# Attention and MLP gradients in one kernel: one masked GpSimd product for the block diagonals, GpSimd preparation, and a third pair of PSUM banks in the last stage

## The chip, the cores and the metric

The kernel runs on one core of a Trainium2 chip. The metric is the device time of one execution in microseconds (us). The times of before are the median of five runs, 505.92 us; the single runs lie between 502.8 and 509.14. The profile is of one more execution, and its instruction times are used below.

The core's engines work on queues of their own and meet only through semaphores. PE is the matrix engine (PEld its weight loads), DVE is VectorE, ACT is ScalarE, POOL is GpSimd, and SP here only issues transfers. Matrix results land in PSUM, eight banks of 2 KB per partition; DVE or ACT must move them to SBUF ("evacuate") before a transfer can write them out.

## The reference

One decode step with two sequences: x is layer-normed, attention over a cached K and V (16 key heads, 32 query heads, 4096 positions of 128) and a gated bilinear MLP run side by side, and their sum with x is the output. The kernel also returns the gradients with respect to x, K, V and the five weights, for a given gradient dy of the output:

```
xn  = (x - mean) / sqrt(var + eps)
q   = xn wq;  p = softmax(q K^T / sqrt(128));  o = p V
out = x + o wo + ((xn w_gate) * (xn w_up)) w_down
```

The large outputs are sums of a few outer products. For one sequence and key head, dV is p^T (dy wo^T) over the two query heads of that key head, and dK is ds^T q with ds the gradient of the scores: 4096 x 128 elements, each a sum of two products. The weight gradients are outer products with two terms, one per sequence: wq from xn and dq (out_4), wo from o and dy (out_5), and the three of the MLP (out_6 to out_8). As much is written as is read: 92.48 MB each way.

The gradient with respect to x passes back through the layer norm with the row sums of dxn and dxn * xn; it and the output are two rows of 576 elements.

## The kernel before

The key heads are taken in four groups of four. A group has four steps (two sequences by two pairs of heads), so there are 16 steps. A step loads two K heads and two V heads of 1 MB each (`kv` tiles of the pool tag `nat`, 12 buffers), transposes them on DVE (tile `X`), forms scores on PE in `ps_sc`, takes the softmax, forms dscores, and contracts with K and V. Beside this run the nine slices of the MLP (`mlp_units`), a few units per step, and at the end of each group `back_units` with the group's weight gradients.

The dK and dV outputs come from `outer_units`. Per head there are four units; a unit fills a pair of PSUM banks with two matmuls of 128x512 and evacuates them into a quarter of a 1 MB tile `so`, and after the fourth POOL issues the write of that tile. The stationary operand is a masked product: `masked` multiplies the rows of p or ds by a 0/1 mask into 128x1024 (`prm`, `dsm`) in one POOL product. The moving operand is the block diagonal `bd`, 128 x (2, 4, 128): partition block a holds `dense` in its place a and zeros elsewhere. `build_bd` makes it: a small matmul, an ACT copy to `dense` (L511), and four POOL copies of 32 partitions (L516) into one of three tiles that were set to zero once at the start (L229 to L231).

PSUM is divided by tags: `m` (two small tiles), `sc` (two tiles for the scores), and `o` (two pairs of banks, `ps_o`, L80). Every outer product of the kernel takes a pair `ps_o` and is evacuated by `evac` (L104), which keeps a running estimate of the load of DVE and ACT and gives each evacuation to the engine that would be done first; `dve()` and `act()` add the estimates of other work. Evacuations have the line L109 on DVE and L112 on ACT, all blocked matmuls the line L93.

The order of the work is that of the program text, filled in by a scheduler that moves instructions of lower priority between those of the main chain; on each engine the order is fixed when the program is built. In the main loop, `slot` takes two outer units after each half of a head (`more(2)`) and side units (`other`). After the last step the remaining outer units (twelve, of the last V and K heads), `back_units` of the last group and `final_units` are left. They alternate: two outer units, then one side unit. `final_units` are: `prepare` (L793: loads x and dy again, converts them to 32 bits and norms x, on DVE), `output` (L807: transposes the sum `acc` and adds x), `rows` (L819: the row sums of `accx` by matmul into a `ps_o` pair, moved by DVE), and `gradient` (L832: nine DVE instructions of 2x576 or less in one chain). `back_units` has `first` (L665, with the matmuls with `wo` at L670, the transposes L678 and `R`), `second` (the contribution of wq to dxn, added to `accx` at L305), eight `outer_o` (L726, tile `sto`), four `outer_q` (L692, tile `stq`) and `outer_qt` (L714, tile `stqt`).

Of the kernel before, what the change touches and what calls it, by code (L numbers as in the profile page):

```python
# [9 lines left out]
ALU = mybir.AluOpType  # L10
AX = mybir.AxisListType
FP32 = mybir.dt.float32
BF16 = mybir.dt.bfloat16
P = 128


def view(t, p0, np_, off, dims):

    (pstep, _), *_ = t.ap
    return bass.AP(t.tensor, t.offset + p0 * pstep + off, [[pstep, np_], *[list(d) for d in dims]])  # L20
# [3 lines left out]
def kernel(  # L24
# [22 lines left out]
    nc = tc.nc  # L47

    Bq, Sq, D = A_x.shape
    _, Hkv, Sk, Dh = A_k_cache.shape  # L50
# [5 lines left out]
    GH = 2 * G  # L56
    NGRP = Hkv // G
# [10 lines left out]
    HD2 = D // 2  # L68

    const = ctx.enter_context(tc.tile_pool(name="const", bufs=1))  # L70
    sb = ctx.enter_context(tc.tile_pool(name="sb", bufs=1))
    ps = ctx.enter_context(tc.tile_pool(name="ps", bufs=1, space=bass.MemoryType.PSUM))
# [7 lines left out]
    def ps_o():  # L80
        return ps.tile([P, 2, 512], FP32, tag="o", bufs=2, name="ps_o")

    class Block:


# [16 lines left out]
    load = {"v": 0.0, "s": 0.0}  # L102

    def evac(out, in_, cols):  # L104
        cv = 0.16 + cols * 0.00104
        cs = 0.19 + cols * 0.00083
        if load["v"] + cv < load["s"] + cs:
            load["v"] += cv
            nc.vector.tensor_copy(out=out, in_=in_)  # L109
        else:  # L110
            load["s"] += cs
            nc.scalar.copy(out, in_)  # L112

    def dve(us):
        load["v"] += us

    def act(us):
        load["s"] += us
# [28 lines left out]
    Q4 = sums("Q4", [[32, 4], [1, 32]])  # L147
    C32 = sums("C32", [[4, 32], [1, 4]])
    maskc = const.tile([P, 8], BF16, name="maskc")
    with nc.allow_low_precision("zeros and ones"):  # L150
        nc.vector.reduce_sum(maskc[:], view(C32[:], 0, P, 0, [[1, 8], [8, 4]]), axis=AX.X)
    mask8 = const.tile([P, 4, 2], FP32, name="mask8")
    nc.vector.tensor_copy(mask8[:], view(Q4[:], 0, P, 0, [[1, 4], [0, 2]]))

# [12 lines left out]
    x_f = sb.tile([2, D], FP32, tag="X", bufs=3, name="x_f")  # L167
    mu = const.tile([2, 1], FP32, name="mu")
# [4 lines left out]
    xn_f = sb.tile([2, D], FP32, tag="nat", bufs=12, name="xn_f")  # L173
# [6 lines left out]
    rstd = const.tile([2, 1], FP32, name="rstd")  # L180
# [8 lines left out]
    xnr = const.tile([P, D], BF16, name="xnr")  # L189
    dyr = const.tile([P, D], BF16, name="dyr")  # L190
    for src, dst in ((dy_bf, dyr), (xn_bf, xnr)):
        o = ps_o()
        for k in range(2):
            nc.tensor.matmul(o[:, k, 0:HD2], lhsT=sel2[:].rearrange("b a m -> b (a m)"),
                             rhs=src[0:2, k * HD2:(k + 1) * HD2], start=True, stop=True)
# [30 lines left out]
    oTs = [const.tile([P, 2, GH, 32], BF16, name=f"oT{i}") for i in range(2)]  # L226
    for t in (*Wms, *Wts, *oTs):
        nc.gpsimd.memset(t[:], 0.0)
    bds = [const.tile([P, 2, 4, Dh], BF16, name=f"bd{i}") for i in range(3)]  # L229
    for r in bds:  # L230
        nc.gpsimd.memset(r[:], 0.0)  # L231
    n_bd = [0]
    nwm = [0]

    rowT = [[const.tile([P, P + 28], BF16, name=f"rowT{t}{i}") for i in range(2)] for t in range(2)]
# [20 lines left out]
    def swtile(shape, name):  # L256
        return sb.tile(list(shape), BF16, tag="st", bufs=5, name=name)
# [243 lines left out]
    def build_bd(st, b, s, t):  # L501

        nc.gpsimd.tensor_copy(
            view(dM[:], 0, P, t * 2 * P, [[P + 2, 2], [4, 32], [1, 2]]),
            view(st["qd"][:], 0, P, (2 if t == 0 else 1) * GH * 2 + 8 * s + b, [[4, 2], [0, 32], [2, 2]]),
        )
        bp = ps_m([P, 2, Dh])
        for x in range(2):
            nc.tensor.matmul(bp[:, x, :], lhsT=dM[:, t, x], rhs=ident[:], start=True, stop=True)
        dense = sb.tile([P, 2, Dh], BF16, tag="dense", bufs=1, name="dense")  # L510
        nc.scalar.copy(dense[:], bp[:])  # L511
        act(0.4)
        bd = bds[n_bd[0] % 3]
        n_bd[0] += 1
        for a in range(4):
            nc.gpsimd.tensor_copy(bd[32 * a:32 * a + 32, :, a, :], dense[32 * a:32 * a + 32])  # L516
        return bd

    def small(name, shape=(P, 1), dtype=FP32, bufs=2):
# [64 lines left out]
    def outer_units(rows, bd, b, l0, oview):  # L584
        m = {}

        def unit(x, cp):
            def f():
                if cp == 0:
                    m["st"] = stile([P, 4, 8, Dh], "so")  # L590
                st = m["st"]
                o = ps_o()
                with Block() as mm:
                    for c in range(2):
                        mm(o[:, c, :], lhsT=rows[:, 2 * cp + c, :], rhs=bd[:, x].rearrange("p a d -> p (a d)"),
                           start=True, stop=True)
                evac(view(st[:], 0, P, 2 * cp * Dh, [[Dh, 2], [8 * Dh, 4], [1, Dh]]),
                     o[:].rearrange("p c (a d) -> p c a d", a=4), 1024)
                if cp == 3:
                    nc.gpsimd.dma_start(oview[b, :, :, l0 + x].rearrange("a m n -> m a n"),  # L600
                                        st[:].rearrange("p a c d -> p a (c d)"))
            return f
        return [unit(x, cp) for x in range(2) for cp in range(4)]
# [56 lines left out]
    def back_units(st):  # L660
        g, wq, wo, oT = st["g"], st["wq"], st["wo"], st["oT"]
        n0 = g * GH * Dh
        m = {}

        def first():  # L665
            yp = ps_m([P, 5, 2])
# [25 lines left out]
        def outer_q(k, A):  # L692
            def f():
                R = m["R"]
                if A == 0:
                    m["st"] = swtile([P, 2, GH * P], "stq")
                st = m["st"]
                o = ps_o()
                with Block() as mm:
                    for dc in range(2):  # L700
                        for aa in range(2):
                            a = 2 * A + aa
                            d0 = (2 * k + dc) * P
                            mm(o[:, aa, 256 * dc:256 * dc + 256], lhsT=xnr[32 * a:32 * a + 32, d0:d0 + P],
                                             rhs=R[32 * a:32 * a + 32, 1].rearrange("p h d -> p (h d)"),
                                             start=True, stop=True)
                evac(view(st[:], 0, P, 512 * A, [[256, 2], [GH * P, 2], [1, 256]]),
                     o[:].rearrange("p a (d n) -> p a d n", d=2), 1024)
                if A == 1:
                    nc.gpsimd.dma_start(out_4[256 * k:256 * k + 256, n0:n0 + GH * P].rearrange("(c p) n -> p c n", p=P),  # L710
                                        st[:])
            return f
# [14 lines left out]
        def outer_o(A, h2, k):  # L727
            def f():
                R = m["R"]
                if h2 == 0 and k == 0:  # L730
                    m["so"] = swtile([P, 4, D], "sto")
                o = ps_o()
                with Block() as mm:
                    for aa in range(2):
                        a = 2 * A + aa
                        mm(o[:, aa, 0:HD2], lhsT=R[32 * a:32 * a + 32, 0, h2, :],
                                         rhs=dyr[32 * a:32 * a + 32, k * HD2:(k + 1) * HD2], start=True, stop=True)
                evac(view(m["so"][:], 0, P, h2 * D + k * HD2, [[2 * D, 2], [1, HD2]]), o[:, :, 0:HD2], D)
                if h2 == 1 and k == 1:
                    r0 = n0 + 4 * A * P  # L740
                    nc.gpsimd.dma_start(out_5[r0:r0 + 4 * P, :].rearrange("(h p) n -> p h n", p=P), m["so"][:])
            return f
# [29 lines left out]
    def end_of_K(st, b, s, K, dsT):  # L772
        t_ps = contract(dsT, K)
        nc.vector.tensor_scalar(st["oT"][:, 1, 4 * s:4 * s + 4, b], t_ps[:], SCALE, None, op0=ALU.mult)
        dve(0.2)
# [14 lines left out]
    def final_units():  # L790
        m = {}

        def prepare():  # L793
            x_b2 = fin([2, D], BF16, "x_b2")
            nc.sync.dma_start(x_b2[:], A_x.rearrange("b s d -> (b s) d"))
            dy_b2 = fin([2, D], BF16, "dy_b2")
            nc.sync.dma_start(dy_b2[:], grad_out.rearrange("b s d -> (b s) d"))
            x_f = m["x"] = fin([2, D], FP32, "x_f2")
            nc.vector.tensor_copy(x_f[:], x_b2[:])
            dy_f = m["dy"] = fin([2, D], FP32, "dy_f")  # L800
            nc.vector.tensor_copy(dy_f[:], dy_b2[:])
            xn_f = m["xn"] = fin([2, D], FP32, "xn_f2")
            nc.vector.tensor_scalar(xn_f[:], x_f[:], mu[:], None, op0=ALU.subtract)
            nc.vector.tensor_scalar(xn_f[:], xn_f[:], rstd[:], None, op0=ALU.mult)
            m["rowf"] = fin([2, 2, D], FP32, "rowf")

        def output():  # L807
# [53 lines left out]
    st = group_front(0, *loaded)  # L861
# [3 lines left out]
    for n in range(NIT):  # L865
        g, b, s = step(n)
# [37 lines left out]
        last = (st, b, s, K, dsT, dsm, bd0)  # L904
        if new:
            st = nxt
    end_of_K(*last[:5])
    outs += outer_units(last[5], last[6], last[1], G * last[0]["g"] + 2 * last[2], okview)
    units = back_units(last[0])
# [34 lines left out]
```

## Time and profile before

| | |
|---|---|
| median of five runs | 505.92 us (502.8 to 509.14) |
| the profiled execution | 503.11 us |
| its span, first to last instruction | 501.3 us |
| busy PE / DVE / ACT / POOL | 388.1 / 352.2 / 333.4 / 254.3 us (77 / 70 / 66 / 51%) |
| read and written | 92.48 MB each, 369 GB/s over the span |
| last matmul of the scores' contraction | about 467 us |
| last evacuation ends | 495.4 us |

"Busy" is the time in which an engine executes; a share of it is a mean over stages, so it does not say what limits a stage. The page cuts the span into 40 slices of 12.5 us; each digit is a busy share in tenths. A row of the timeline gives the start, the duration, engine, line, operation, the tile written and the tile read, how many instructions are merged, and in brackets the idle time before them and what ended it. In other views one row is a group of instructions of one line and shape. On an engine that works in a pipeline, the next instruction may start slightly before the row of the one before it ends.

### The profile page before, as it was taken

To read this page: it belongs to the slowest core of one execution; us is meant where nothing else is said; L and a number is where in the kernel's file an instruction comes from. 1 tells how busy PE (TensorE), PEld (TensorE's weight loads), DVE (VectorE), ACT (ScalarE), POOL (GpSimd) and SP (SyncE) were. 2 spreads that over 40 slices of the span, in tenths; PEclk is the share of its full clock that TensorE was granted. 3 is DMA by queue.
4 is the path that set the end of the run, shared out by engine and by line. 5 is a ranking of instruction groups with operands and counts; after the bars stand their busy time and mean duration, and the time that the engine had idled before them with its cause. 6 is when DMAs were issued, how large, how long until landed. Compare 5 with 4: busy or idle time off the path is not lost.

```text
span 501.3 us, 17208 instructions
## 1 busy us (share of the span) xinstructions
PE 388.1 (77%) x7337; PEld 266.5 (53%) x7417; DVE 352.2 (70%) x626; ACT 333.4 (66%) x488; POOL 254.3 (51%) x500
## 2 busy tenths in 40 slices
PE   2678848878989758877878879858977888889862
PEld 1565526656657536554645547535655655556520
DVE  6686653787877835866966776867758774799574
ACT  4244866867884766858745696857746587778763
POOL 5235354466546544564636356454645447384613
PEclk9975987999997977979986997979978997989995
DMA  7997998999999999999999999999999999995675
GB/s 248 385 396 277 363 418 294 419 418 411 410 422 404 417 417 321 420 417 413 385 384 396 399 419 347 388 419 404 403 380 410 396 419 355 393 387 189 228 268 210
DMA packets 52900, 186.07 MB, mean 371 GB/s; under 512 B 4140, under 2 KB 19128, under 8 KB 44632
## 3 DMA queue, kind: packets, MB, share of 16 engines
q1 hardware_dynamic: 28392, 92.49, 48.2%
q0 software_dynamic: 24432, 92.48, 46.7%
q8 instruction: 58, 0.95, 0.7%
q14 instruction: 18, 0.15, 0.1%
HBM read 92.48 MB, written 92.48 MB: 369 GB/s over the span
## 4 chain that ended last, share of the span: by engine, by line
PE 35%; DMA 22%; ACT 18%; DVE 12%; issue 6%; POOL 1%; POOLq 0%; ACTq 0%; DVEq 0%
DMA out_dram<-so 15%; ACT so L112 14%; PE ps_o L93 13%; PE ps_m L93 11%; PE ps_sc L93 6%; DVE X L121 5%; DMA kv<-in_A_k_cache_dram 4%; DMA out_dram<-stq 3%; DVE so L109 2%; DVE Xw L121 1%; ACT sto L112 1%; ACT stw L112 1%; PE ps_m L574 1%; PE ps_sc L552 1%; DVE stw L109 1%
## 5 line engine op out<-in xcount | busy, mean ns | idle before, releaser
L112 ACT CAST so<-ps_o 128x1024 bf16<-128x1024 f32 x227 | 220.9, 1024 | 60.2 <-PE ps_o L93 29.6
L121 DVE STREAM_TRANSPOSE X<-kv 128x1024 f32<-128x1024 f32 x128 | 155.5, 1225 | 19.6 <-PE ps_sc L93 12.3
L93 PEld LDWEIGHTS <-X 128*128 128x128 bf16 x2048 | 81.2, 103 | 27.4 <-DVE X L121 13.4
L600 POOL DMA_DIRECT2D out_dram<-so x64 | 49.7, 777 | 88.3 <-ACT so L112 33.7
L93 PE MATMUL ps_sc<-W,X 128*128 128x64 bf16 (+1 forms) x2048 | 88.9, 200 | 6.2 <-DVE X L121 3.8
L93 PE MATMUL ps_o<-bd,prm 128*128 128x512 bf16 x209 | 74.1, 424 | 17.5 <-DVE stw L109 6.5
L93 PE MATMUL ps_o<-bd,dsm 128*128 128x512 bf16 x223 | 70.4, 392 | 17.2 <-ACT so L112 12.5
L516 POOL COPY bd<-dense 32x256 bf16<-32x256 bf16 x128 | 50.9, 397 | 13.3 <-ACT dense L511 8.8
L109 DVE CAST so<-ps_o 128x1024 bf16<-128x1024 f32 x29 | 35.1, 1211 | 16.4 <-PE ps_o L93 12.3
L93 PE MATMUL ps_m<-kv,rowT 128*32 128x128 bf16 x2048 | 43.2, 250 | 2.8 <-issue 1.9
L93 PEld LDWEIGHTS <-prm 128*128 128x128 bf16 x256 | 22.6, 107 | 36.9 <-issue 25.6
L93 PEld LDWEIGHTS <-dsm 128*128 128x128 bf16 x256 | 21.7, 98 | 36.6 <-issue 26.9
L93 PEld LDWEIGHTS <-rowT 128*32 128x32 bf16 x2048 | 36.8, 113 | 5.4 <-issue 3.6
L112 ACT CAST stw<-ps_o 128x1024 bf16<-128x1024 f32 x27 | 26.7, 1033 | 18.6 <-DMA out_dram<-so 11.1
L496 POOL COPY W<-rep 32x16 bf16<-32x16 bf16 x128 | 24.9, 195 | 24.9 <-PE ps_sc L93 14.3
L580 POOL TENSOR_TENSOR prm<-pr,maskc 128x1024 bf16<-128x1024 bf16 x16 | 30.2, 1887 | 14.3 <-DVE pr L630 14.0
L580 POOL TENSOR_TENSOR dsm<-ds,maskc 128x1024 bf16<-128x1024 bf16 x16 | 30.3, 1894 | 12.7 <-DVE ds L651 12.1
L93 PE MATMUL ps_o<-hb,xnr 32*128 32x128 bf16 (+1 forms) x360 | 19.9, 236 | 15.9 <-ACT so L112 7.5
L93 PEld LDWEIGHTS <-xnr 32*128 32x128 bf16 (+1 forms) x440 | 14.6, 99 | 33.0 <-issue 29.3
L571 ACT COPY o_sb<-ps_m 128x128 f32<-128x128 f32 x32 | 8.7, 271 | 35.1 <-PE ps_m L93 34.9
L121 DVE STREAM_TRANSPOSE Xw<-wgu 128x1152 f32<-128x1152 f32 x18 | 24.6, 1370 | 4.2 <-PE ps_sc L93 4.1
L396 POOL DMA_DIRECT2D out_dram<-stw x18 | 13.7, 762 | 25.4 <-ACT stw L112 14.3
(179 smaller groups left out, 585.1 us busy)
## 6 DMA issues: line engine op xcount, KB each, us to landing
out_dram<-so POOLq DMA_DIRECT2D x64, 1024.0 KB, 11.4
kv<-in_A_k_cache_dram SPq DMA_DIRECT2D x32, 1024.0 KB, 13.9
kv<-in_A_v_cache_dram SPq DMA_DIRECT2D x32, 1024.0 KB, 14.4
out_dram<-stw POOLq DMA_DIRECT2D x18, 512.0 KB, 9.8
wd<-in_B_w_down_dram SPq DMA_DIRECT2D x9, 576.0 KB, 6.9
out_dram<-std POOLq DMA_DIRECT2D x9, 576.0 KB, 13.0
wo<-in_A_wo_dram SPq DMA_DIRECT2D x4, 1152.0 KB, 10.1
wgu<-in_B_w_gate_dram SPq DMA_DIRECT2D x9, 512.0 KB, 15.5
```

Source lines behind the costliest of these rows:

```text
L93: ins = nc.tensor.matmul(*args, **kwargs)
L109: nc.vector.tensor_copy(out=out, in_=in_)
L112: nc.scalar.copy(out, in_)
L121: nc.vector.transpose(out, in_)
L396: nc.gpsimd.dma_start(out[0:512, f0:f0 + FS].rearrange("(c p) n -> p c n", p=P), st[:])
L496: nc.gpsimd.tensor_copy(view(W[t][:], 32 * a, 32, 48 + 4 * a, [[2 * WW, 4], [WW + 2, 2], [1, 2]]), view(st["rep"][:], 32 * a, 32, t * 4 * ...
L516: nc.gpsimd.tensor_copy(bd[32 * a:32 * a + 32, :, a, :], dense[32 * a:32 * a + 32])
L552: nc.tensor.transpose(s_ps[:], s_sb[:], identf[:])
L571: nc.scalar.copy(o_sb[:], o_ps[:])
L574: nc.tensor.matmul(t_ps[:], lhsT=o_sb[:], rhs=RV[:].rearrange("p x r -> p (x r)"), start=True, stop=True)
L580: nc.gpsimd.tensor_tensor(m[:], view(rows[:], 0, P, 0, [[0, 8], [1, P]]), view(maskc[:], 0, P, 0, [[1, 8], [0, P]]), ALU.mult)
L600: nc.gpsimd.dma_start(oview[b, :, :, l0 + x].rearrange("a m n -> m a n"), st[:].rearrange("p a c d -> p a (c d)"))
```

## The change

There are four edits. The block diagonal becomes one POOL product of `dense`, read four times over, with a new mask `maskq` (128x4), written into a rotating tile of three buffers instead of the three zeroed ones. `prepare` runs on POOL, with the two norming instructions merged into one. After the last step a list `ending` is filled and the load estimates are set to zero; from then on every third pair is taken from the two `sc` banks as two single tiles (`ps_pair`), and such a pair is evacuated in two halves, each given to an engine on its own (`evac_pair`). And in the last group the tiles `stq` and `sto` come from the tag `nat` instead of `st`.

```diff
+    pairs_made = [0]
+    ending = []
+    def ps_pair():
+        pairs_made[0] += 1
+        if ending and pairs_made[0] % 3 == 0:
+            o = [ps.tile([P, 512], FP32, tag="sc", bufs=2, name="ps_x") for _ in range(2)]
+            return [t[:] for t in o], None
+        o = ps_o()
+        return [o[:, 0, :], o[:, 1, :]], o
...
+    def evac_pair(out, o, whole, cols, view_in=lambda t: t):
+        if whole is not None:
+            evac(out(None), view_in(whole[:]), cols)
+        else:
+            for a in range(2):
+                evac(out(a), view_in(o[a]), cols // 2)
...
+    maskq = const.tile([P, 4], BF16, name="maskq")
+    nc.vector.tensor_copy(maskq[:], Q4[:])
...
-    bds = [const.tile([P, 2, 4, Dh], BF16, name=f"bd{i}") for i in range(3)]
-    for r in bds:
-        nc.gpsimd.memset(r[:], 0.0)
-    n_bd = [0]
...
-        bd = bds[n_bd[0] % 3]
-        n_bd[0] += 1
-        for a in range(4):
-            nc.gpsimd.tensor_copy(bd[32 * a:32 * a + 32, :, a, :], dense[32 * a:32 * a + 32])
+        bd = sb.tile([P, 2, 4, Dh], BF16, tag="bd", bufs=3, name=f"bd{t}")
+        nc.gpsimd.tensor_tensor(bd[:], view(dense[:], 0, P, 0, [[Dh, 2], [0, 4], [1, Dh]]),
+                                view(maskq[:], 0, P, 0, [[0, 2], [1, 4], [0, Dh]]), ALU.mult)
...
-                o = ps_o()
+                o, whole = ps_pair()
                 with Block() as mm:
                     for c in range(2):
-                        mm(o[:, c, :], lhsT=rows[:, 2 * cp + c, :], rhs=bd[:, x].rearrange("p a d -> p (a d)"),
+                        mm(o[c], lhsT=rows[:, 2 * cp + c, :], rhs=bd[:, x].rearrange("p a d -> p (a d)"),
...
+        stq = nat if g == NGRP - 1 else swtile
...
-            nc.vector.tensor_copy(x_f[:], x_b2[:])
+            nc.gpsimd.tensor_copy(x_f[:], x_b2[:])
...
-            nc.vector.tensor_copy(dy_f[:], dy_b2[:])
+            nc.gpsimd.tensor_copy(dy_f[:], dy_b2[:])
...
-            nc.vector.tensor_scalar(xn_f[:], x_f[:], mu[:], None, op0=ALU.subtract)
-            nc.vector.tensor_scalar(xn_f[:], xn_f[:], rstd[:], None, op0=ALU.mult)
+            nc.gpsimd.tensor_scalar(xn_f[:], x_f[:], mu[:], rstd[:], op0=ALU.subtract, op1=ALU.mult)
...
+    ending.append(1)
+    load["v"] = load["s"] = 0.0
     end_of_K(*last[:5])
```

`outer_q` and `outer_o` take `ps_pair` and `evac_pair` in the same way as `outer_units`; `outer_qt`, `output` and `rows` keep `ps_o`.

More of the change, by code (lines that the diff above doesn't have):

```diff
@@ L591, in f @@
                 st = m["st"]
-                o = ps_o()
+                o, whole = ps_pair()
                 with Block() as mm:
                     for c in range(2):
-                        mm(o[:, c, :], lhsT=rows[:, 2 * cp + c, :], rhs=bd[:, x].rearrange("p a d -> p (a d)"),
+                        mm(o[c], lhsT=rows[:, 2 * cp + c, :], rhs=bd[:, x].rearrange("p a d -> p (a d)"),
                            start=True, stop=True)
-                evac(view(st[:], 0, P, 2 * cp * Dh, [[Dh, 2], [8 * Dh, 4], [1, Dh]]),
-                     o[:].rearrange("p c (a d) -> p c a d", a=4), 1024)
+                evac_pair(lambda c: view(st[:], 0, P, (2 * cp + (c or 0)) * Dh,
+                                         ([[Dh, 2]] if c is None else []) + [[8 * Dh, 4], [1, Dh]]), o, whole, 1024,
+                          lambda x: x.rearrange("p c (a d) -> p c a d" if whole is not None else "p (a d) -> p a d", a=4))
                 if cp == 3:
@@ L695, in f @@
                 if A == 0:
-                    m["st"] = swtile([P, 2, GH * P], "stq")
+                    m["st"] = stq([P, 2, GH * P], "stq")
                 st = m["st"]
-                o = ps_o()
+                o, whole = ps_pair()
                 with Block() as mm:
@@ L703, in f @@
                             d0 = (2 * k + dc) * P
-                            mm(o[:, aa, 256 * dc:256 * dc + 256], lhsT=xnr[32 * a:32 * a + 32, d0:d0 + P],
+                            mm(o[aa][:, 256 * dc:256 * dc + 256], lhsT=xnr[32 * a:32 * a + 32, d0:d0 + P],
                                              rhs=R[32 * a:32 * a + 32, 1].rearrange("p h d -> p (h d)"),
                                              start=True, stop=True)
-                evac(view(st[:], 0, P, 512 * A, [[256, 2], [GH * P, 2], [1, 256]]),
-                     o[:].rearrange("p a (d n) -> p a d n", d=2), 1024)
+                evac_pair(lambda aa: view(st[:], 0, P, 512 * A + 256 * (aa or 0),
+                                          ([[256, 2]] if aa is None else []) + [[GH * P, 2], [1, 256]]), o, whole, 1024,
+                          lambda x: x.rearrange("p a (d n) -> p a d n" if whole is not None else "p (d n) -> p d n", d=2))
                 if A == 1:
@@ L730, in f @@
                 if h2 == 0 and k == 0:
-                    m["so"] = swtile([P, 4, D], "sto")
-                o = ps_o()
+                    m["so"] = stq([P, 4, D], "sto")
+                o, whole = ps_pair()
                 with Block() as mm:
@@ L735, in f @@
                         a = 2 * A + aa
-                        mm(o[:, aa, 0:HD2], lhsT=R[32 * a:32 * a + 32, 0, h2, :],
+                        mm(o[aa][:, 0:HD2], lhsT=R[32 * a:32 * a + 32, 0, h2, :],
                                          rhs=dyr[32 * a:32 * a + 32, k * HD2:(k + 1) * HD2], start=True, stop=True)
-                evac(view(m["so"][:], 0, P, h2 * D + k * HD2, [[2 * D, 2], [1, HD2]]), o[:, :, 0:HD2], D)
+                so = m["so"]
+                evac_pair(lambda aa: view(so[:], 0, P, h2 * D + k * HD2 + 2 * D * (aa or 0),
+                                          ([[2 * D, 2]] if aa is None else []) + [[1, HD2]]), o, whole, D,
+                          lambda x: x[:, :, 0:HD2] if whole is not None else x[:, 0:HD2])
                 if h2 == 1 and k == 1:
```

## The prediction

> **What bounds the kernel now.** I read three views in turn: the page's slices, the busy time in two stretches, and the instructions in order of time in the last 33 us. First the slices:
>
> ```profile
> DMA  7997998999999999999999999999999999995675
> GB/s 248 385 396 277 363 418 294 419 418 411 410 422 404 417 417 321 420 417 413 385 384 396 399 419 347 388 419 404 403 380 410 396 419 355 393 387 189 228 268 210
> ```
>
> Each digit is 12.5 us. From slice 6 to slice 36 the DMA engines are at 9 or more; the last four slices (from 451 us) are not. The two stretches:
>
> ```profile
> 0.00:450.00 450.00, 353.55 (x6792) 247.09 (x6866) 318.66 (x567) 300.91 (x445) 232.97 (x470) 0.88 1.00 388
> 450.00:501.30 51.30, 34.58 (x545) 19.38 (x551) 33.52 (x60) 32.45 (x43) 21.33 (x31) 0.87 0.62 227
> ```
>
> Columns: busy us of PE, PEld, DVE, ACT, POOL, then clock, DMA share, GB/s. For 450 us the transfers are full (share 1.00), so engine work there is covered. In the last 51 us the share is 0.62 and no engine is full: PE 67%, DVE 65%, ACT 63%. There the hand-over between engines sets the time:
>
> ```profile
> 474.26 1.22 DVE L109 CAST so<-ps_o 128x1024 bf16<-128x1024 f32 x1 [0.20 <-PE ps_o L93]
> 475.25 1.93 ACT L112 CAST so<-ps_o 128x1024 bf16<-128x1024 f32 x2 [0.68 <-PE ps_m L93]
> ...
> 476.32 0.59 PE L93 MATMUL ps_o<-bd,dsm 128*128 128x512 bf16 x2 [0.19 <-ACT so L112]
> ...
> 476.95 1.23 DVE L109 CAST so<-ps_o 128x1024 bf16<-128x1024 f32 x1 [1.23 <-PE ps_o L93]
> ```
>
> PE fills a pair of banks from 476.32, its evacuation starts 0.63 later, and PE has the banks back when that ends. One pair cycles in 0.63 + 1.02 + 0.04 = 1.69 us on ACT, 1.90 on DVE; ACT then waits 0.68 for the next. Two pairs give 0.85 to 0.95 us each, which is what a third pair could shorten. But DVE has other work here:
>
> ```profile
> 483.49 1.23 DVE L109 CAST so<-ps_o 128x1024 bf16<-128x1024 f32 x1
> 484.63 0.73 DVE L836 TENSOR_REDUCE m<-rowf 2x1 f32<-2x576 f32 x1
> ...
> 486.03 0.73 DVE L109 CAST sto<-ps_o 128x576 bf16<-128x576 f32 x1
> ...
> 490.64 0.73 DVE L851 TENSOR_TENSOR dx_bf<-t,dy_f 2x576 bf16<-2x576 f32 x1
> ```
>
> The gradient runs from 484.63 to 491.37 with four `sto` evacuations between its steps; without these (four steps of 0.67) it is 4.1 us long.
>
> **Part 1: the block diagonal by one product.** 128 copies go, 32 products come; three 0.95 us memsets at 4.5 to 7.2 us go too, where POOL has nothing to do until 13.65, so they return nothing.
>
> ```profile
> L580 POOL TENSOR_TENSOR prm<-pr,maskc x16: 1883/1887/1892, 40.2 to 463.6; 128x1024 bf16<-128x1024 bf16 x16
> ```
>
> ```profile
> L516 POOL COPY bd<-dense x128: 386/393/560, 35.2 to 467.6; 32x256 bf16<-32x256 bf16 x128
> ```
>
> (Minimum, median, maximum ns.) The existing masked product has the new one's size, type and two broadcast inputs: 1.89 us, against 4 x 0.393 = 1.57, at most 1.70 to 1.72 from start to end. So +0.17 to +0.32 us each, 32 times: 5.4 to 10.2 us more POOL work on 254.3 in 501.3. It lies beside full transfers; no PE wait in the list is put down to bd, so I cost it at 0. If the cover went, it would be +6 us (32 x 0.19), and a product at twice the row's time is not excluded by any row (+2.1 x 32 = 67 us of POOL work, still under 65% busy). Behind bd on POOL stand the `so` writes, 0.2 us later each.
>
> The Trainium skill, GPSIMD Engine Reference, section 2.1, puts a two-input product at about 2.5 cycles per element; at its 1.2 GHz that is an estimate of 2.13 us, so the sum would be about +14 us of POOL work against 1.89 us measured here. That speaks against this part. The row decides.
>
> **Part 2: preparation on GpSimd.** The four DVE instructions (L799, L801, L803, L804: 0.45, 0.65, 0.64, 0.75 us at 449.35 to 453.0) go; three come on POOL, behind `dsm`:
>
> ```profile
> 448.62 2.01 POOL L516 COPY bd<-dense 32x256 bf16<-32x256 bf16 x4
> 450.72 1.97 POOL L580 TENSOR_TENSOR dsm<-ds,maskc 128x1024 bf16<-128x1024 bf16 x1
> 454.93 0.79 POOL L600 DMA_DIRECT2D out_dram<-so  x1 [2.24 <-ACT stt L112]
> ```
>
> On DVE I find no gain: the `so` at 451.05 needs the pair PE began at 450.07, the one at 453.26 waits for PE, the X transpose at 453.75 waits 0.32 for PE. Next late is PE itself. Bound: 0 to 0.5 us. On POOL no row shows these three. Below: a 576-element copy by the slope from 32x16 (0.195) to 32x256 (0.393) is 0.66 us, three are 2.0; above: 576/1024 of 1.89 is 1.06, three are 3.2. POOL is idle 2.24 us here. I take 2.4, nearest the copies: the `so` write of 454.93, the two `stt` writes and bd behind it go back by about 0.4 us (0 to 1.0). DMA share is 0.06 at 452 to 456, and that bd is first needed at 467.77 against an end near 459.3. Price 0. What the loads L795 and L797 deliver was issued at 429.0 and 434.5.
>
> These rows show bd copies at 2.01 instead of 1.70 and `dsm` at 1.97 instead of 1.89 beside those DVE instructions. The Trainium skill, SBUF — State Buffer, "Who interferes with whom", explains such rows: an SBUF copy in a two-port mode, or two SBUF inputs, holds a port pair that GpSimd shares. By that rule part 2 returns 0.4 us of POOL time. X transposes beside a POOL copy took 1.22 us, alone 1.23, so most of DVE's work does not meet it.
>
> **Part 3: the end.** In the changed program the order on PE differs only from 468.4 us on. From there 17 `so`, 8 `sto`, 4 `stq` and 2 `stqt` evacuations remain. Every third pair comes from the `sc` banks and is evacuated in two halves: 4 of `so`, 3 of `sto`, 1 of `stq`. A whole costs 1.02 on ACT and 1.23 on DVE; a half of 512 columns 0.58 and 0.69 (the 64x512 `stqt` rows), one of 288 about 0.40 and 0.45 (between the 256- and 512-column rows).
>
> - ACT gets 8 whole `so` and 6 halves for 12 whole (-0.6), 3 and 3 halves of `sto` for 4 (+0.55), 2 and a half of `stq` for 2 (+0.6), one `stqt` for 2 (-0.6): 17.5 us as before.
> - DVE keeps its 5 `so` and gets 2 halves (+1.4), 2 and 3 halves of `sto` for 4 (-0.1), one and a half of `stq` for 2 (-0.5), a `stqt` (+0.7): +1.4 on 20.0 (all its groups from 467.8 to 496).
>
> So the sum grows by 1.4 us, nothing passes from one engine to the other, and only overlap can gain. I followed the new orders with these times, each step against the trace:
>
> 1. A `prm` pair in the `sc` banks slips in ahead of the L670 matmuls (0.6 us later), so ACT's first whole of the `so` tile of head 1, before at 472.57 to 473.57, ends at 474.2.
> 2. From there ACT runs nearly without waiting: half, whole, half, two wholes, two halves, whole, two halves of `so`: 4 x 1.0 + 6 x 0.58 = 7.5 us, and about 0.3 of waits: 482.0.
> 3. PE is in order, and the first `sto` pair in the `sc` banks waits for those last halves, so the row sums (L823) start at 482.35 (before: 481.61); their results are out at 484.2, the last `so` evacuation on DVE at 485.4 (before 484.71).
> 4. The whole gradient now stands on DVE ahead of all its `sto` evacuations: 485.4 + 4.1 = 489.5 (before 491.37). A half of the first `sto` pair waits behind it; the third pair's banks come back only at 489.8, and PE stands from about 486.5 until then, with what is left of `sto` and all of `stq` queued behind it.
> 5. DVE then has 0.4 + 0.7 + 0.4 + 0.7 + 0.4 + 1.2 + 0.7 + 0.7 = 5.2 us: about 494.7 (before 494.68). POOL's last write is issued at 495.8 to 496.0 (before 495.89); from there to the end of the span is 5.4 us, as before.
>
> What is gained in the `so` stretch goes into the block at 486.5. Bounds: -1.5 (wait of step 4 shorter, no X-pair delay) to +1.5 (each hand-over 0.1 us longer). Sum: 0 + 0 - 0.2 = span 501.1, own time 502.9 instead of 503.11 (1.8 us lie around the span). The median of the five runs, 505.92, is 2.8 us above the profiled run; I forecast against it: **505.7 us**.
>
> **Rivals.**
>
> - *The third pair pays.* With three pairs in turn the rate is 0.6 us a pair, and DVE becomes the bound. If DVE were dense from 467.88, with 21.4 us, it would end at 489.3 instead of 494.68: -5.4, about 500.5; half of it 503.2. For it: PE waits behind evacuations in every cycle of 475 to 482. Against it: step 4. It decides if the first `sto` halves get out before the gradient.
> - *POOL starves the writes* (slower). In the body the 32 products delay the write issues; with no backlog in the write queue each 0.19 us is on the path: +6.0, 511.9. For it: POOL waits 33.7 us for ACT ahead of `so` writes, so it has no work ahead. Against it: DMA share 0.99 to 1.03 from 100 to 450 us. It decides when that share falls under 1.
> - *It does less than it says.* The gradient block costs more than the overlap gave, with the third pair idle behind it: PE stands 3.3 us of which 1.5 to 3 are not recovered: 507 to 509.
>
> **How the numbers follow.** Forecast (504.2 to 507.2) 0.60; third pair pays 0.18, half of it beyond 1%; POOL starves 0.10; does less 0.12. The five runs shown spread from 502.8 to 509.14, so about 1% is what a measurement can tell from no change. Range: half the dense-DVE gain and the spread of runs below, the third rival and a little above: 501.3 to 509.8. Faster 0.13 (0.09 and 0.04 for the spread), slower 0.13 (0.10 and 0.03), same 0.74.
>
> **What would show it.** Right: the same 450 us at share 1.00; bd products of 1.89 us; PE idle for about 3 us near 486 to 490 with DVE in the gradient (L858 to L873 of the changed kernel); last POOL write near 496. Wrong: DVE evacuations of `sto` inside the gradient, a last write before 493, or a DMA share under 0.95 in the body.

## The result and the profile after

The changed kernel is a little slower: 507.85 us median (503.5 to 513.98, 41 runs) against 504.39 us for the kernel before (499.9 to 509.14, 76 runs). The ratio is 1.0066, with a 95% interval of 1.0051 to 1.008, so about 3.3 us are lost where 0.2 were to be gained. Executions more than 1.5% above the fastest of their kernel are left out of the ratios here and below.

The page of the kernel after, with the slices that answer to those of before:

```profile
span 504.9 us, 17102 instructions
...
DMA  8998998999999999999999999999999999995575
GB/s 249 381 396 289 372 417 288 421 420 409 401 420 406 418 417 323 419 415 394 347 382 394 415 414 350 406 414 393 374 363 415 409 419 362 399 362 180 224 279 187
```

The two stretches, in the columns used before (busy PE, PEld, DVE, ACT, POOL, then clock, DMA share, GB/s):

```profile
0.00:450.00 450.00, 351.35 (x6731) 244.06 (x6807) 318.49 (x563) 300.71 (x444) 237.11 (x376) 0.89 1.00 386
450.00:504.90 54.90, 36.35 (x611) 21.59 (x618) 34.76 (x65) 31.83 (x48) 27.76 (x29) 0.84 0.62 225
```

Both have the DMA shares of before, 1.00 and 0.62. What is new shows when the last step is taken as a mark: its masked product `prm`, the last of the `prm` products on POOL (the kernel before first):

```profile
463.60 1.88 POOL L580 TENSOR_TENSOR prm<-pr,maskc 128x1024 bf16<-128x1024 bf16 x1 [2.76 <-DVE pr L630]
```

```profile
466.10 1.88 POOL L597 TENSOR_TENSOR prm<-pr,maskc 128x1024 bf16<-128x1024 bf16 x1 [2.68 <-DVE pr L648]
```

In these two executions 2.5 us are lost ahead of the mark, in a body whose transfers look as full as they were. From one execution to the next the mark itself moves by several microseconds (460.9 to 467.4 in eleven profiled kernels with copies), so one pair of traces does not show how much of this is the change. From the mark on the order of the instructions decides: up to POOL's last write the times repeat to about 0.1 us in kernels with the same end.

| us | before | after |
|---|---|---|
| last `prm` product starts | 463.6 | 466.1 |
| from there to the end of POOL's last write instruction | 32.84 | 32.69 |
| from there to the end of the span | 4.86 | 6.11 |

So POOL's last write is issued 0.15 us earlier against the mark, and the span ends 1.1 us later against the mark. The rows of the end, in order of time, POOL first and then the rest (idle time and what ended it in brackets):

```profile
487.57 0.75 POOL L618 DMA_DIRECT2D out_dram<-so  x1 [4.94 <-ACT sto L124]
493.08 0.75 POOL L764 DMA_DIRECT2D out_dram<-sto  x1 [4.75 <-DVE sto L121]
494.72 0.75 POOL L764 DMA_DIRECT2D out_dram<-sto  x1 [0.89 <-DVE sto L121]
496.27 1.42 POOL L730 DMA_DIRECT2D out_dram<-stq  x2 [0.80 <-DVE stq L121]
497.68 1.11 POOL L745 DMA_DIRECT2D out_dram<-stqt  x2
```

```profile
486.94 0.73 DVE L858 TENSOR_REDUCE m<-rowf 2x1 f32<-2x576 f32 x1
...
490.74 0.75 DVE L873 TENSOR_TENSOR dx_bf<-t,dy_f 2x576 bf16<-2x576 f32 x1
491.42 0.44 DVE L121 CAST sto<-ps_x 128x288 bf16<-128x288 f32 x1
...
491.91 0.39 PE L105 MATMUL ps_x<-dyr,R 32*128 32x288 bf16 x1 [4.41 <-DVE sto L121]
...
492.58 0.64 ACT L124 CAST sto<-ps_o 128x576 bf16<-128x576 f32 x1 [4.22 <-PE ps_o L105]
```

This is the block that step 4 of the prediction describes. The gradient stands on DVE from 486.94; the half of the first `sto` pair waits behind it until 491.42; PE stands 4.41 us for its banks, ACT 4.22 us for PE. Two `sto` writes and the four of `stq` and `stqt`, 2.3 MB together, are then issued within 5.7 us. The transfers of that stretch, in the columns used above, and then those of the kernel before at the same distance from its mark:

```profile
491.00:493.00 2.00, 1.06 (x7) 0.31 (x7) 1.89 (x4) 0.42 (x1) 0.00 (x0) 0.50 0.31 118
493.00:495.00 2.00, 1.82 (x16) 0.42 (x16) 1.63 (x3) 1.70 (x4) 1.04 (x2) 0.50 0.31 111
495.00:497.00 2.00, 1.32 (x8) 0.47 (x7) 1.91 (x3) 1.42 (x2) 1.20 (x3) 0.50 0.90 316
497.00:499.00 2.00, 0.10 (x2) 0.00 (x0) 0.00 (x0) 0.58 (x1) 1.79 (x3) 0.50 0.95 336
499.00:501.00 2.00, 0.00 (x0) 0.00 (x0) 0.00 (x0) 0.00 (x0) 0.00 (x0) 0.50 1.06 354
```

```profile
489.00:491.00 2.00, 1.02 (x10) 0.35 (x10) 2.00 (x4) 1.07 (x2) 0.60 (x1) 0.50 0.66 240
491.00:493.00 2.00, 1.24 (x12) 0.25 (x7) 1.60 (x2) 1.26 (x2) 0.75 (x1) 0.50 0.63 222
493.00:495.00 2.00, 1.12 (x8) 0.25 (x4) 1.23 (x1) 0.87 (x3) 1.09 (x2) 0.50 0.87 315
495.00:497.00 2.00, 0.00 (x0) 0.00 (x0) 0.00 (x0) 0.41 (x1) 1.45 (x3) 0.50 0.82 279
497.00:499.00 2.00, 0.00 (x0) 0.00 (x0) 0.00 (x0) 0.00 (x0) 0.00 (x0) 0.50 0.61 215
```

After the change the DMA share is 0.31 for the four microseconds around the end of PE's wait and then 0.90 to 1.06 for six; before, it lies between 0.61 and 0.87 throughout. The writes come later and closer together.

### The profile page after: what moved, and what is told of

It is laid out like the page before. It is cut to its first block, busy times and chain, and to the rows that moved or that the text cites. A ratio compares the mean times of both kernels' runs of the same rounds, so it can differ in the third digit from the quotient of the medians.

```text
span 504.9 us, 17102 instructions
## 1 busy us (share of the span) xinstructions
PE 387.7 (77%) x7337; PEld 265.6 (53%) x7417; DVE 353.3 (70%) x627; ACT 332.5 (66%) x492; POOL 264.9 (52%) x404
## 5 line engine op out<-in xcount | busy, mean ns | idle before, releaser
L124 ACT CAST so<-ps_o 128x1024 bf16<-128x1024 f32 x223 | 217.4, 1024 | 59.1 <-PE ps_o L105 30.2
L105 PEld LDWEIGHTS <-X 128*128 128x128 bf16 x2048 | 79.9, 102 | 29.2 <-DVE X L141 16.8
L105 PE MATMUL ps_o<-bd,prm 128*128 128x512 bf16 x208 | 75.6, 433 | 17.9 <-DVE stw L121 6.0
L105 PE MATMUL ps_o<-bd,dsm 128*128 128x512 bf16 x216 | 67.9, 390 | 16.0 <-ACT so L124 10.6
L532 POOL TENSOR_TENSOR bd<-dense,maskq 128x1024 bf16<-128x1024 bf16 x32 | 60.7, 1897 | 9.9 <-ACT dense L529 9.4
L105 PEld LDWEIGHTS <-dsm 128*128 128x128 bf16 x256 | 21.6, 99 | 34.8 <-issue 25.3
```

The lines of the kernel that those rows point to most:

```text
L105: ins = nc.tensor.matmul(*args, **kwargs)
L532: nc.gpsimd.tensor_tensor(bd[:], view(dense[:], 0, P, 0, [[Dh, 2], [0, 4], [1, Dh]]), view(maskq[:], 0, P, 0, [[0, 2], [1, 4], [0, Dh]]), ...
```

## Experiments

Ratios are to the kernel before, run beside the kernel in question, with 95% intervals; 12 runs each unless said otherwise. "Tail" is the time from the start of the last `prm` product to the end of the span in the profiled run: 37.70 us before, 38.80 after.

### One part at a time

`e1_bd` has only the product, `e2_prep` only the preparation on POOL, `e3_end` only the edits of the end, `e4_no_bd` all but the product (its block diagonals go into the three zeroed tiles again).

```diff
 e4_no_bd, against the changed kernel
-        nc.gpsimd.tensor_tensor(bd[:], view(dense[:], ...), view(maskq[:], ...), ALU.mult)
+        for a in range(4):
+            nc.gpsimd.tensor_copy(bd[32 * a:32 * a + 32, :, a, :], dense[32 * a:32 * a + 32])
```

> Only the block diagonal by one masked POOL product; preparation and end as before. Theory B (the loss is in the body: the longer product holds up the writes behind it on POOL, since at the last steps the changed kernel is already 2.5 us behind): about +2.5 us, ratio 1.005. Theory E (the loss is made after the last step, by the blocked evacuations and the writes bunched at the end; the 2.5 us in the body are the spread between executions): 0 to +0.5 us, ratio 1.000 to 1.001, with the last POOL write as far from the end of the span as before (4.9 us).

> Only the preparation on POOL. In the changed kernel its three instructions took 3.5 us (0.65, 0.66, 2.29) and put the write of so behind them back by about 1 us. Theory E: that write and the bd behind it have slack, 0 (ratio 0.999 to 1.001). Rival P: the late write and bd push the last steps, +1.0 us (ratio 1.002).

> Only the third pair, the halves, the reset loads and the nat tiles of the last group; block diagonals by copies and preparation on DVE. Theory E: nearly all of the loss, +2.5 to +3.5 us (ratio 1.005 to 1.007); ACT idle about 4 us ahead of a sto, and the last POOL write 5.5 to 6.2 us before the end of the span. Theory B: 0 to +1 us (ratio 1.000 to 1.002).

> The changed kernel with the block diagonal by four copies again. Theory E: as the changed kernel, +3 us (ratio 1.006). Theory B: +0.5 to +1 us (ratio 1.001 to 1.002).

| | ratio | tail, us |
|---|---|---|
| e1_bd (6 runs) | 1.0118 (1.0073 to 1.0162) | 37.72 |
| e2_prep | 1.0012 (0.9983 to 1.0042) | 37.65 |
| e3_end | 1.0026 (0.9992 to 1.006) | 38.57 |
| e4_no_bd | 1.0038 (1.0005 to 1.007) | 38.57 |

Theory E is half wrong. The end costs what the tails say, 0.9 to 1.1 us, and not 2.5 to 3.5; the preparation alone costs nothing that these runs can tell. The product alone stands above the whole change, though the intervals just overlap. One stall shows in its rows, in order of time:

```profile
453.22 1.91 POOL L512 TENSOR_TENSOR bd<-dense,maskq 128x1024 bf16<-128x1024 bf16 x1
...
453.92 3.37 DVE L796 CAST x_f<-x_b 2x576 f32<-2x576 bf16 x1 [0.20 <-PE ps_m L93]
...
455.07 1.90 POOL L577 TENSOR_TENSOR dsm<-ds,maskc 128x1024 bf16<-128x1024 bf16 x1
```

The copy `x_f` took 0.45 us in the kernel before. Here it stands across two masked products that follow each other, and ends just after the second. The last two `prm` products lie 20.36 us apart instead of 18.35, 2.0 us more. This distance is 18.15 to 18.40 us in most of the kernels run here, but 16.8 in `g1_product_first` and 19.1 in `h2_product_back` below, so that the stall makes all of the 2.0 us is likely and not shown. In the changed kernel this copy runs on POOL, so there the stall does not arise. That is what the preparation on POOL can be good for, and only with the product.

The same happens to another instruction in both kernels, the scaling of q (L459 before, L477 after):

```profile
120.34 1.48 DVE L459 TENSOR_SCALAR qd<-qd 128x16 bf16<-128x16 bf16 x1
```

```profile
L477 DVE TENSOR_SCALAR qd<-qd x4: 172/1020/3308, 12.8 to 356.4; 128x16 bf16<-128x16 bf16 x4
```

The first row is the kernel before, from its timeline; the second the kernel after (minimum, median, maximum ns of its four). It takes 0.17 us alone, 1.0 to 1.5 beside a product, and 3.31 across two. One `pr` (L648) at 38 us, which took 0.30 us beside the four copies of the kernel before, takes 1.53 us beside a `bd` product in the same way. The Trainium skill's SBUF — State Buffer, "Who interferes with whom", has the rule: a copy, cast or scaling on VectorE that runs in a two-port mode shares a port pair with GpSimd, and whichever of the two comes first holds the pair for its whole instruction while the other waits. The rows beside one product agree; the rows of 3.31 and 3.37 us show besides that the wait went on across a second product right behind the first.

### Is it POOL's time, or these stalls? And is it the gradient block?

```diff
 f1_qd_ps, against the changed kernel
-        nc.vector.tensor_scalar(qd[:, 2], qd[:, 0], SCALE, None, op0=ALU.mult)
+        nc.vector.tensor_scalar(qd[:, 2], qp[:], SCALE, None, op0=ALU.mult)
 f2_copies_plus, against e4_no_bd
-        for a in range(4):
+        for a in (0, 1, 2, 3, 3):
 f3_plan, against the changed kernel (f4_no_bd_plan: against e4_no_bd)
+            dve(1.5)          # at the end of output()
+            dve(1.1 + 4.1)    # at the end of gradient()
```

> The changed kernel, with the scaled q (L477) computed from the PSUM result qp instead of from its SBUF copy qd. Theory L (the product costs time because a VectorE instruction that reads and writes SBUF stands until the masked product next to it has ended: this one took 0.17 us alone, 1.02 and 3.31 beside products): the instruction takes about 0.2 us at all four places, and the kernel gets back a part of its loss, at most 1.8 + 0.9 + 0.9 us: ratio 1.002 to 1.006. Theory T (it is POOL's longer time itself): ratio as the changed kernel, 1.0066.

> The changed kernel with the block diagonal by copies, and the fourth copy made twice: five copies, about 2.0 us of POOL for each block diagonal, as much as the product (1.90 us) or more. Theory T: as the changed kernel or above, ratio 1.006 to 1.008. Theory L: short instructions let VectorE in between; as with four copies, ratio 1.003 to 1.004.

> The changed kernel, with the planner's load of VectorE raised by 1.5 us in output and by 5.2 us in gradient, so that ScalarE gets nearly all evacuations of sto. Theory E (the gradient block on VectorE ahead of the halves is what eats the gain of the third pair): no wait of PE of 3 us at 487 to 491, last POOL write 2 to 3 us earlier against the start of the dsm product of the last step, ratio 1.001 to 1.003. Rival (the end is bounded by the hand-over of banks or by the writes, not by that block): 1.006 to 1.007.

> The same with the block diagonal by four copies: preparation on POOL, third pair, and the planner told of the final stage. If both theories hold, faster than both kernels: 500 to 503 us, ratio 0.994 to 0.999. If the end is bounded otherwise: as without the product, 1.004.

| | ratio | tail, us |
|---|---|---|
| f1_qd_ps | 1.0058 (1.0025 to 1.0091) | 38.67 |
| f2_copies_plus | 1.0006 (0.997 to 1.0041) | 38.71 |
| f3_plan | 0.9991 (0.9965 to 1.0017) | 36.09 |
| f4_no_bd_plan | 0.9949 (0.992 to 0.9978) | 36.01 |

POOL's time is not the cause. In `f2_copies_plus` the block diagonals keep POOL busy longer than the products do in the changed kernel, and its ratio, 1.0006 with an upper bound of 1.0041, stays below the interval of the changed kernel (1.0051 to 1.008). First `f2_copies_plus`, then the changed kernel, from the groups of POOL by shape (busy us, mean ns):

```profile
L536 POOL COPY bd<-dense 32x256 bf16<-32x256 bf16 x160 | 63.5, 397 | 13.0 <-ACT dense L531 7.1
```

```profile
L532 POOL TENSOR_TENSOR bd<-dense,maskq 128x1024 bf16<-128x1024 bf16 x32 | 60.7, 1897 | 9.9 <-ACT dense L529 9.4
```

The stall of `qd` is gone in `f1_qd_ps` (0.16 to 0.17 us at all four places), but its ratio is not told apart from that of the changed kernel.

The gradient block is what ate the gain of the third pair. Once the planner counts the final stage as DVE's, ACT takes all `sto` evacuations but one, and the tail is 36.0 to 36.1 us: 2.6 to 2.7 shorter than in the same kernels without that count, and 1.6 to 1.7 shorter than before. ACT in `f4_no_bd_plan`, in order of time:

```profile
483.61 0.64 ACT L124 CAST sto<-ps_o 128x576 bf16<-128x576 f32 x1
484.14 0.72 ACT L124 CAST sto<-ps_x 128x288 bf16<-128x288 f32 x2
484.73 1.22 ACT L124 CAST sto<-ps_o 128x576 bf16<-128x576 f32 x2
485.79 0.77 ACT L124 CAST sto<-ps_x 128x288 bf16<-128x288 f32 x2
486.37 0.73 ACT L124 CAST sto<-ps_o 128x576 bf16<-128x576 f32 x1
486.90 0.81 ACT L124 CAST sto<-ps_x 128x288 bf16<-128x288 f32 x2
488.91 1.01 ACT L124 CAST stq<-ps_o 128x1024 bf16<-128x1024 f32 x1 [1.20 <-PE ps_x L105]
```

Six rows follow each other without a wait, where the changed kernel has one of 4.22 us. Its first `sto` write is issued at 486.24, 23.4 us after the mark (before 25.3, after 27.0). At 0.9949 this version is faster than both kernels; run a second time (`i2_copies` below) it gave 0.9976, with an interval that reaches 1.

### Which products cost, and what the third pair is worth

```diff
 g1_product_first / g2_product_late, against f4_no_bd_plan
...
+        if n_bd[0] <= 8:      # g2_product_late: > 8
+            nc.gpsimd.tensor_tensor(bd[:], view(dense[:], ...), view(maskq[:], ...), ALU.mult)
+        else: the four copies
 g3_no_third, against f4_no_bd_plan
-        if ending and pairs_made[0] % 3 == 0:
+        if False:
 g4_end_plan, against f4_no_bd_plan: the preparation on VectorE, as before
```

> The version with copies, preparation on POOL, third pair and the planner told of the final stage (ratio 0.9949), but the first 8 of the 32 block diagonals (steps 0 to 3) by the product. Both long VectorE stalls beside products (1.5 us at 38 us, 3.3 us at 120 us) lie in these steps. Theory L (those stalls are what the product costs): ratio 0.998 to 1.000, as with all 32 products (0.9991). Theory D (each product costs a little, spread over the body): 0.995 to 0.997.

> The same with the product in the other 24 (steps 4 to 15). Theory L: ratio 0.994 to 0.996, as with copies. Theory D: 0.997 to 0.999.

> The version with copies and the planner told of the final stage, but no third pair: every pair from the o banks, whole evacuations. If the third pair brings the gain once the gradient block is out of its way: 1.5 us or more slower than with it, ratio 0.998 to 1.000, with ScalarE waiting 0.7 us for each pair as before. If the planner's numbers alone bring it: 0.995, as with the third pair.

> The version with copies, third pair and the planner told, with the preparation back on VectorE. If the preparation on POOL is worth nothing (as run alone: 1.0012): ratio 0.995. If it gives back the 2.5 us of VectorE: 0.998 to 1.000.

| | ratio | tail, us |
|---|---|---|
| g1_product_first | 0.9997 (0.9963 to 1.0031) | 35.96 |
| g2_product_late | 1.0014 (0.9976 to 1.0051) | 36.07 |
| g3_no_third | 0.9988 (0.9951 to 1.0025) | 37.49 |
| g4_end_plan | 0.9959 (0.9926 to 0.9991) | 35.99 |

The third pair is worth 1.5 us of tail (37.49 against 36.01) once nothing blocks it. Without it, ACT waits for each pair as in the kernel before; `g3_no_third`:

```profile
477.98 1.01 ACT L124 CAST so<-ps_o 128x1024 bf16<-128x1024 f32 x1 [0.68 <-PE ps_o L105]
479.67 1.01 ACT L124 CAST so<-ps_o 128x1024 bf16<-128x1024 f32 x1 [0.68 <-PE ps_o L105]
```

The preparation on POOL again shows no difference with copies. On the product both theories missed: the first eight and the last 24 each stand about as high as all 32, so no proportion to the number of products shows, though intervals of about 0.0035 either way could hide one. `g2_product_late` says the most about the stalls. It does not contain the two longest, and all its VectorE instructions together take 348.1 us against 348.7 in `f4_no_bd_plan`, no longer than with copies; yet it stands 0.0055 above `g4_end_plan`, which ran beside it, with an uncertainty of 0.005 by the two intervals. That speaks against the VectorE stalls as the cost of the product.

### Or is it the place of the tiles?

The new mask takes 8 bytes per partition near the start of SBUF, and moves the tiles behind it on by 32 bytes: `kv` and `so`, which the transfers fill and empty, begin at a multiple of 64 bytes in every kernel with the product so far, and 32 beyond one in every kernel without it. That could be the cause in place of the product.

```diff
 h1_copies_shift, against f4_no_bd_plan; h4_before_shift, against the kernel before
+    maskq = const.tile([P, 4], BF16, name="maskq")
+    nc.vector.tensor_copy(maskq[:], Q4[:])
 h2_product_back, against f3_plan; h3_after_back, against the changed kernel
-    maskq = const.tile([P, 4], BF16, name="maskq")
+    maskq = const.tile([P, 20], BF16, name="maskq")
...
 i1_product_in_place, against f4_no_bd_plan: all 32 by the product, into the three zeroed tiles
+    maskcq = const.tile([P, 12], BF16, name="maskc")
+    maskc, maskq = maskcq[:, 0:8], maskcq[:, 8:12]
...
 i2_copies: f4_no_bd_plan again
```

> The version with copies and the planner told (ratio 0.9949), with the 8-byte mask maskq added and filled but not used: all tiles of the transfers begin 32 bytes later, at a multiple of 64. Theory A (the place of the tiles is what costs, not the product): ratio 0.998 to 1.001. Rival (the product costs): 0.994 to 0.996.

> The changed kernel with the planner told (ratio 0.9991), with the mask widened to 40 bytes, so that the tiles of the transfers begin 32 bytes beyond a multiple of 64 as in the kernel before; all 32 products stay. Theory A: 0.993 to 0.996. Rival: 0.998 to 1.000.

> The changed kernel, only the mask widened to 40 bytes. Theory A: 1.002 to 1.004 (what the end alone costs). Rival: 1.0066 as the changed kernel.

> The kernel before, with the 8-byte mask added and filled but not used. Theory A: 1.004 (2 us slower with no other change). Rival: 1.000.

> The version with preparation on POOL, third pair and the planner told, with all 32 block diagonals by the product; every tile of the transfers stands where it stands in the version with copies. If the product itself costs (theory P): 0.3 to 0.5% above the run with copies, ratio 0.998 to 1.002. If the place of the tiles costs (theory A): equal to the run with copies, 0.994 to 0.997.

> The same version with copies, its program as before at 0.9949, on the same chip as the run with products: 0.993 to 0.997 under both theories.

| | ratio | to be compared with |
|---|---|---|
| h1_copies_shift | 0.9987 (0.9961 to 1.0014) | f4_no_bd_plan 0.9949, i2_copies 0.9976 |
| h2_product_back | 1.0031 (0.9993 to 1.0068) | f3_plan 0.9991 |
| h3_after_back | 1.0039 (1.0004 to 1.0074) | changed kernel 1.0066 |
| h4_before_shift | 1.0010 (0.9981 to 1.0039) | 1 |
| i1_product_in_place | 1.0001 (0.9968 to 1.0034) | i2_copies 0.9976 |
| i2_copies | 0.9976 (0.9943 to 1.0008) | f4_no_bd_plan 0.9949 |

`h1_copies_shift` and `h3_after_back` came out as the theory of the place had it, `h2_product_back` and `h4_before_shift` as its rival: moving the tiles back made one of two kernels faster and the other slower, and the shift alone did 0.001 to the kernel before. So no effect of the place stands out. At equal addresses the product stands 0.0025 above the copies, and the two intervals overlap.

No single pair settles what the product costs, but those that ran side by side all point one way. The version with products stands above that with copies by 0.0052 (`f1_qd_ps` and `f2_copies_plus`), 0.0042 (`f3_plan` and `f4_no_bd_plan`), 0.0038 and 0.0055 (the two `g` versions and `g4_end_plan`), 0.0044 (`h2_product_back` and `h1_copies_shift`, whose places are exchanged) and 0.0025 (`i1_product_in_place` and `i2_copies`). In the `g` versions and in `i1_product_in_place` the product writes into the three zeroed tiles, so the loss does not need the rotating tile either. The means of all with the same end:

| | copies | products |
|---|---|---|
| end as changed | 1.0038, 1.0006, 1.0026: mean 1.0023 | 1.0066, 1.0058, 1.0039: mean 1.0054 |
| planner told | 0.9949, 0.9976, 0.9959, 0.9987: mean 0.9968 | all 32: 0.9991, 1.0031, 1.0001: mean 1.0008 |

The difference is 0.0031 and 0.0040, or 1.6 and 2.0 us, each with an uncertainty of about 1.3 us by the intervals of its runs; the tail is equal to 0.4 us in each row. So the product costs, and it costs in the body. The mark says the same: in the profiled executions it lies at 464.8 us on average in the eleven kernels with copies and at 466.7 in the seven with 32 products (464.1 to 470.2). Single executions scatter by about 2 us there, and at the steps before, the difference wanders between -0.9 and 1.5 us, so the traces do not show where in the body the time goes.

## Why the prediction was wrong

The measured median lies inside the range given, but the direction was missed, and the reasons given for no change were half right. That the median lies inside is no merit: the range was as wide as the spread of single runs, and the forecast started from a median of five runs, 505.92, that lies 1.5 us above that of the 76. The -0.2 us of the sum does not follow from its own steps either, which put POOL's last write at 495.8 to 496.0 against 495.89 before, with the same time behind it.

**Part 1 is the step that failed.** "It lies beside full transfers; no PE wait in the list is put down to bd, so I cost it at 0." The product cost about 1.6 to 2.0 us. Its own duration was right (1.90 us for 1.89), and its POOL time is indeed covered, as five copies show. The share of 1.00 in the body was taken as full cover; it was not enough. All the signs named for being right came: a share of 1.00, products of 1.90 us, a PE wait beside the gradient, and the last POOL write at 495.7 us once the 2.5 us are taken off. None of them tells how long the body takes.

The step left out what a long instruction on POOL does to another engine. One such effect is shown, and it is not one of semaphores, through which alone the engines were said above to meet: the instruction can hold up VectorE, and the trace of before had it, `qd<-qd` at 1.48 us beside a product against 0.17 alone. The prediction went by X transposes beside a copy, which are not held up (1.22 and 1.23 us), and took that for most of VectorE's work. But these stalls are not shown to be the cost. The rival "POOL starves the writes" had the right place and the wrong mechanism and price (+6).

What stays open is how the loss comes about in the body. Stalls of 1.2 and 1.8 us are shown in the first four steps of the changed kernel, but the kernel with products only in the later steps loses no VectorE time against copies and is no faster for it, and eight products stand about as high as 32. Time on POOL, the rotating tile and the place of the tiles are excluded or not supported.

**Part 2** was cost at 0, and alone shows no cost. Its POOL price was outside the bounds: 0.65, 0.66 and 2.29 us, 3.6 in all against an upper bound of 3.2; the norming with two scalars is 3.5 times a copy of the same size. It has an effect that the prediction did not see: with the product, it takes a 3.37 us stall out of the last steps.

**Part 3** was right in its steps and wrong in the last term. Taken from the mark (after minus 2.5 us), the walk stands against the trace like this:

| us | predicted | measured (points in time less 2.5) |
|---|---|---|
| last `so` evacuation on DVE ends | 485.4 | 484.5 |
| gradient ends | 489.5 | 489.0 |
| PE stands for the third pair's banks | 3.3 | 4.4 |
| DVE's last evacuation ends | 494.7 | 494.4 |
| POOL's last write starts | 495.8 to 496.0 | 495.7 |
| from there to the end of the span | 5.4 | 6.7 |

The mis-sized term is the last: "as before". Counted from the end of POOL's last write instruction, the span lasts 6.11 us more against 4.86 before, 1.25 us longer: the block that holds `sto` back also holds its writes back, and 2.3 MB are then issued in 5.7 us. How far the block alone makes this time is not separated; it is 4.8 to 4.9 us in the kernels without a third pair, 5.4 to 5.7 with it and the planner told, and 5.9 to 6.1 with the end as changed. Less the 0.15 us by which the last write comes earlier against the mark, the end loses 1.1 us. With the 1.6 to 2.0 of the product this makes 2.7 to 3.1 us of the 3.3 measured (interval 2.6 to 4.0).

The rival "The third pair pays" named the point from which it decides, and the runs confirm it: with the `sto` evacuations out of the gradient's way the tail is 2.6 to 2.7 us shorter than with them in it, and 1.6 to 1.7 shorter than before. The price named was 2.7 to 5.4 us against before. The rival "It does less than it says" came nearest in time (507 to 509), though it put the whole loss on the gradient block, which has about 1.1 us of it.

## What to carry to other kernels

An engine whose total time is covered can still cost time, here about 1.6 to 2.0 us by a way that stays open. One thing to ask is how long its single instructions are and which short instruction of another engine has to wait for one; that shows in the maxima of the groups, not in their means. A planner that hands out work by estimated loads must be told of the chains that it does not place itself; until it was, the further buffer here only moved the wait. And the last writes are part of the path: here, issued later and closer together, they left 6.1 us instead of 4.9 from the last issue to the end.

## What the runs showed of the hardware

- A 128x16 VectorE scaling within SBUF took 0.17 us alone, 1.0 to 1.5 beside one 1.9 us GpSimd product and 3.31 across two; a 2x576 copy 0.45 and 3.37. With its source in PSUM the scaling took 0.16 to 0.17 at all four places, beside products too.
- On GpSimd a 2x576 copy took 0.65 us and a subtraction and multiplication with two scalars per partition 2.29 us; VectorE needed 0.50 us for each half of the latter in `e1_bd`, with POOL idle beside it, and 0.64 and 0.75 in the kernel before, beside copies and a product on POOL.
- From the last `prm` product to POOL's last write, kernels with the same end repeat to about 0.1 us (32.84 and 32.85 us in the four that keep the old end), and from there to the end of the span to about 0.3, while the mark itself moves by several microseconds. Taking it as a start separated 1 us effects in single profiles.
